# A GLU block beside memory attention on one core: the 64-row tail of each gate-up product held back and run as pairs on two halves of the TensorE array

## The chip, the core and the metric

The kernel runs on one core of a Trainium2 chip. A core has a matrix engine (TensorE, here PE, with its weight loads PEld), a vector engine (VectorE, DVE), a scalar engine (ScalarE, ACT), GpSimd (POOL) and SyncE (SP), whose queue issues most transfers between device memory and SBUF, the working memory of 128 partitions. Matmul results go to PSUM, which is used here as eight banks of 128 partitions by 512 float32. The metric is the time of one execution in microseconds on the device, smaller being better.

## The reference

```python
xn = _layernorm(x)
return x + _A_ref(xn, wq, wk, wv, wo, beta) + _B_ref(xn, w_gate, w_up, w_down)

# _B_ref: gated GLU, x [2048, 448], w_gate and w_up [448, 1792], w_down [1792, 448]
h = sigmoid(xn @ w_gate) * (xn @ w_up)
return h @ w_down
```

`_A_ref` is causal attention of 16 heads of 28 in four segments of 512 tokens, with a running memory of keys and values from the segments before, mixed by a learned gate and projected by `wo`. Everything is float32.

## The kernel before

Each float32 operand of a large product is split into a high part, in the type `float32r`, and the low rest. A product is then high by high, high by low and low by high. The contraction of 448 rows is three chunks of 128 and one of 64. The chunk of 64 is stored twice, one copy below the other, in a tile of 128 partitions: `xs[b][:, 3, :]` has the high part of the last 64 rows in partitions 0 to 63 and the low part in partitions 64 to 127, and the weights have their tail rows twice. So `TERMS` (line 53) has 11 matmuls: nine of the three full chunks, `(3, 3)`, which does high by high and high by low for the tail in one matmul, and `(3, 7)`, which multiplies the low weights with the tail. The tokens are four blocks of 512 (`b`).

The front of the program normalises the input, transposes it (`transpose_high`, `transpose_low`), and makes values, keys and queries. From then on two streams share the engines:

- `gated()` is the GLU. It takes the 14 slices of 128 hidden columns two at a time (`FG = 2`, from `f0`), and for each pair goes over the four token blocks: 28 group-blocks. A group-block has four slots, gate and up of slice `f0`, then gate and up of slice `f0 + 1`. A slot is one product of 11 matmuls of 128x512 into one PSUM bank (line 240). Gates go to the two banks tagged `gu`, ups to the two tagged `p`. After each up (slot 1 and slot 3) the gate is evaluated: ACT takes the tanh (line 248), DVE multiplies it with the up (249, which frees the `p` bank), ACT takes the high part (251) and DVE the low part (252) into `hh`.
- The products with `w_down` (`down`, line 161) wait in the list `todo`. After every slot one of them is popped: six matmuls of 128x448 (line 166) into a bank, and a DVE addition into `acc` (line 169), which frees the bank. The four downs of a group-block (`t` = 0 to 3) use the banks `pd`, `gu`, `pd`, `gu`.
- `attention()` runs in steps between them: score matmuls `st` (line 597, banks `s`), their copy on ACT, masking on POOL, maxima and subtraction on DVE, exponentials on ACT, and per unit of four heads the product `pa` with the values (line 672, the one bank `m`), which DVE transposes out of PSUM (line 675). The `pa` matmuls have 32 output columns each and four of them sit side by side in the array.

The order of PE and of SP's queue is written out by the program; the orders of DVE, ACT and POOL are made by the framework's scheduler. Every `yield` in `gated()` and `project()` lets a number of attention steps pass, spread evenly over all yields.

Weights of a slice come as one transfer of gate and up (`load_up`, tile `raw`, 128x1024, two buffers) and one of down (`load_down`, tile `rawd`, one buffer), and are split by ACT and DVE (`ready_up`, `ready_down`). The dictionary `ahead` says after which block and slot of a group each of these is issued.

After the GLU, `project()` multiplies the attention's output with `wo` and stores; what is left in `todo` runs there from `rest`.

Of the kernel before, what the change touches and what calls it, by code (L numbers as in the profile page):

```python
# [9 lines left out]
F32 = mybir.dt.float32  # L10
F32R = mybir.dt.float32r
AF = mybir.ActivationFunctionType
ALU = mybir.AluOpType
# [3 lines left out]
P = 128  # L17
D = 448
# [3 lines left out]
NB = 4  # L22
L = 512
NT = 4
F = 1792
NF = F // P
# [7 lines left out]
FG = 2  # L34
# [15 lines left out]

HIGH, LOW_X, LOW_W = ([(a + c, w + c) for c in range(3)] for a, w in ((0, 0), (4, 0), (0, 4)))
EARLY = [HIGH + LOW_X + [(3, 3)] + LOW_W + [(3, 7)], HIGH + LOW_W + LOW_X + [(3, 3), (3, 7)]]
TERMS = [t for c in range(3) for t in ((c, c), (c, 4 + c), (4 + c, c))] + [(3, 3), (3, 7)]
KS = 3 * DH
MANUAL = {mybir.EngineType.PE, mybir.EngineType.SP}
# [6 lines left out]
def kernel(  # L62
# [18 lines left out]
    xs = [keep.tile([P, 7, L], F32R, name=f"xs{b}") for b in range(NB)]  # L81
    acc = [keep.tile([P, NT, D], F32, name=f"acc{b}") for b in range(NB)]

    def split(hi, lo, src):
        A.activation(hi, src, AF.Copy)
        V.tensor_sub(lo, src, hi.bitcast(F32))
# [13 lines left out]
    def transpose_low(p3, dst, t):  # L100
        tok = slice(t * P, (t + 1) * P)
        V.tensor_sub(dst[:, 4:7, tok], p3[:, 0:3], dst[:, 0:3, tok].bitcast(F32))
        V.tensor_sub(dst[64:, 3, tok], p3[64:, 3], dst[64:, 3, tok].bitcast(F32))

    def transpose_split(pt, src, dst, t):
        transpose_low(transpose_high(pt, src, dst, t), dst, t)

    def x_block(b):
        return x[b * L:(b + 1) * L, :].rearrange("(t p) d -> p t d", p=P)
# [5 lines left out]
    def bank(name, tag):  # L115
        return ps.tile([P, L], F32, name=name, tag=tag, bufs=banks[tag])
# [22 lines left out]
    mid = ctx.enter_context(tc.tile_pool(name="mid", bufs=3, reuse_waits="tile"))  # L139
# [7 lines left out]
    def two_k(name):  # L147
        return mid.tile([P, L], F32, name=name, tag="2k", bufs=2)
# [10 lines left out]
    def gated():  # L159

        def down(b, hs, wd, t, tag="pd"):
            tok = slice(t * P, (t + 1) * P)
            mms = [(h[:, a, tok], wd[f][:, w, :]) for f, h in hs for a, w in ((0, 0), (0, 1), (1, 0))]
            pd = bank("pd", tag)
            for n, (l, r) in enumerate(mms):
                T.matmul(pd[:, :D], l, r, start=n == 0, stop=n == len(mms) - 1)  # L166
                if n == 2:
                    yield
            V.tensor_add(acc[b][:, t, :], pd[:, :D], acc[b][:, t, :])  # L169
            yield  # L170

        raw_up, raw_down, wgu, wdn = {}, {}, {}, {}

        def load_up(f):

            raw_up[f] = mid.tile([P, 1024], F32, name="raw", bufs=2)
            if f < NF:
                nc.sync.dma_start(raw_up[f], w_ffn[f][:, :1024])
            else:
                nc.sync.dma_start(raw_up[f][:, :2 * D], w_o[:, 2 * D * (f - NF):2 * D * (f - NF + 1)])  # L180

        def load_down(f, tag="rawd"):
            raw_down[f] = (mid.tile([P, 1024], F32, name="raw", bufs=2)[:, :D] if tag == "raw" else
                           mid.tile([P, D], F32, name="rawd", bufs=1))
            nc.sync.dma_start(raw_down[f], w_ffn[f][:, 1024:])

        def ready_up(f):
            wgu[f] = eight_k(F32R, "wgu")
            split_weights(wgu[f], raw_up[f].rearrange("p (c n) -> p c n", c=4))

        def ready_down(f):
            wdn[f] = late_pair("wdn")
            split(wdn[f][:, 0, :], wdn[f][:, 1, :], raw_down[f])

        def ready_out(h):
            wo[h] = eight_k(F32R, "wo").rearrange("p c n -> p (c n)")
# [12 lines left out]
        for f0 in range(0, NF, FG):  # L209


            ahead = {}
            if f0 == 0:
                ahead[0, 0] = lambda: (load_down(1, "raw"), ready_up(1))
                ahead[0, 2] = lambda: load_up(2)
                ahead[1, 3] = lambda: load_up(3)
            if f0 + FG < NF:
                ahead[1, 2] = lambda: ready_up(f0 + 2)
                if f0 > 0:
                    ahead[2, 1] = lambda: ready_down(f0 + 2)  # L220
                ahead[2, 3] = lambda: load_down(f0 + 3)
                ahead[2, 2] = lambda: load_up(f0 + 4)
                ahead[3, 2] = lambda: ready_up(f0 + 3)
                ahead[3, 3] = lambda: ready_down(f0 + 3)
                if f0 > 0:
                    ahead[0, 2] = lambda: (load_up(f0 + 3), load_down(f0 + 2))
            else:

                ahead[0, 2] = lambda: load_up(f0 + 3)
                ahead[1, 2] = lambda: ready_out(0)  # L230
                ahead[3, 2] = lambda: ready_out(1)
            for b in range(NB):
                hs = []
                for f in range(f0, f0 + FG):
                    pgu = []
                    for side in range(2):
                        slot = 2 * (f - f0) + side
                        dst = bank("pgu", ("gu", "p")[side])
                        for n, (a, w) in enumerate(TERMS):
                            T.matmul(dst, wgu[f][:, w, side * P:(side + 1) * P], xs[b][:, a, :],  # L240
                                     start=n == 0, stop=n == len(TERMS) - 1)
                            if n in (3, 7):
                                yield
                        pgu.append(dst)
                        if side == 1:

                            sg = two_k("sg")
                            A.activation(sg, pgu[0], AF.Tanh, scale=0.5)  # L248
                            V.scalar_tensor_tensor(sg, sg, 1.0, pgu[1], op0=ALU.add, op1=ALU.mult)  # L249
                            hh = four_k(F32R, "hh")  # L250
                            A.activation(hh[:, 0, :], sg, AF.Copy, scale=0.5)  # L251
                            V.scalar_tensor_tensor(hh[:, 1, :], sg, 0.5, hh[:, 0, :].bitcast(F32),  # L252
                                                   op0=ALU.mult, op1=ALU.subtract)
                            hs.append((f, hh))
                        yield
                        if todo and f0 + b > 0:
                            yield from todo.pop(0) or ()
                        if (b, slot) in ahead:
                            ahead[b, slot]()
                end = f0 + FG == NF and b == NB - 1  # L260
                todo += [down(b, hs, wdn, t, ("pd", "s" if end else "gu")[t % 2]) for t in range(NT)]
        rest.extend(todo)


    N_FFN = NF // FG * NB * 20 - 12


    with tc.tile_pool(name="front", bufs=2) as sb, tc.manual_schedule(engines=FRONT):
# [49 lines left out]
            return xn  # L318

        def turn(b, t, xn):  # L320
            transpose_split(bank("pt", "s"), xn, xs[b], t)

        def value_terms(b, t, pv, terms, n0=0, n1=len(TERMS)):
            for n in range(n0, n1):
# [112 lines left out]
            p3[t] = transpose_high(bank("pt", "s"), xn[t], xs[0], t)  # L437

        def turn_low(t):
            transpose_low(p3[t], xs[0], t)  # L440

        def normalised(t):
            xn[t] = normalise(0, t, *rstd(*st[t], y[t])[0])
# [49 lines left out]
        for b in range(NB):  # L493
# [24 lines left out]
            for k, c in enumerate((3, 4, 5, 6, 0, 1, 2) if last else range(7)):  # L518
# [215 lines left out]
    def project():  # L734

        def split_tokens(b, t):
            o3 = sums[b][:, :, t * P:(t + 1) * P]
            A.activation(xs[b][:, 0:4, t * P:(t + 1) * P], o3, AF.Copy)
            transpose_low(o3, xs[b], t)

        def out_weights(w):
            at = 2 * D * (w // 4) + D * (w % 2)
# [76 lines left out]
```

## Time and profile before

| What | Value |
|---|---|
| Time, median of 3 runs | 697.93 us (696.47, 697.93, 700.5) |
| Profiled execution, first to last instruction | 697.6 us |
| PE, PEld busy | 690.0 us, 567.7 us |
| DVE busy | 570.2 us |
| ACT, POOL busy | 343.6 us, 148.5 us |
| Gate-up products (line 240) | 1232 matmuls of 128x512 |
| Down products (line 166) | 672 matmuls of 128x448 |
| TensorE clock granted | 0.997 of full |

Matmuls overlap in the pipeline, so the busy time of one (398 ns for a 128x512 one) is longer than the distance from its start to the next one's. Rates are read from start to start. DVE, ACT and POOL work through their queues in order, so an instruction that waits holds up what stands behind it on its engine.

### The profile page before, as it was taken

The page shows a single profiled execution, that of the slowest core. Times are in us where ns is not written, and L with a number is a line of the kernel's source. Part 1 is how long each engine was busy: PE and PEld are TensorE (multiplying, and loading weights), DVE is VectorE, ACT ScalarE, POOL GpSimd, SP SyncE. Part 2 cuts the span into 40 slices and gives each one's busy share as a digit, 9 for nine tenths or more (in the row PEclk, how much of TensorE's full clock was granted, in tenths as well). Part 3 has the DMA queues.
Part 4 walks back from the last instruction along what each step waited for, and adds up shares of the span by engine and source line. Part 5 has one row for each costly group of instructions (what it writes and reads, how often), then busy time and mean ns, then how long its engine had stood idle before and what let it go on. Part 6 is the DMA issues. An engine that isn't in the chain of part 4 may idle for free.

```text
span 697.6 us, 10438 instructions
## 1 busy us (share of the span) xinstructions
PE 690.0 (99%) x3594; PEld 567.7 (81%) x3594; DVE 570.2 (82%) x994; ACT 343.6 (49%) x563; POOL 148.5 (21%) x349
## 2 busy tenths in 40 slices
PE   8989999999999999999999999999999999999997
PEld 7878878777878787877878778787787878778897
DVE  6665687658789898988898889998898889889863
ACT  5646646344455455543655446455644555446320
POOL 4400010101222131322222222132221322222000
PEclk9999999999999999999999999999999999999999
DMA  7833545687222423234323343324242432333342
GB/s 265 320 130 149 201 185 211 226 300 224 70 77 65 120 86 85 48 113 108 78 58 96 70 128 66 98 56 114 74 108 66 95 70 60 86 94 88 91 152 105
DMA packets 45797, 84.37 MB, mean 121 GB/s; under 512 B 6321, under 2 KB 20401, under 8 KB 45233
## 3 DMA queue, kind: packets, MB, share of 16 engines
q1 hardware_dynamic: 42736, 76.37, 35.3%
q0 software_dynamic: 3008, 7.34, 5.2%
q8 instruction: 28, 0.46, 0.3%
q14 instruction: 25, 0.20, 0.1%
HBM read 51.05 MB, written 32.64 MB: 120 GB/s over the span
## 4 chain that ended last, share of the span: by engine, by line
PE 94%; DMA 2%; DVE 1%; ACT 1%; SPq 0%; issue 0%; ACTq 0%
PE pgu L240 42%; PE pd L166 20%; PE pp L344 9%; PE st L597 5%; PE pa L672 5%; PE po L756 5%; PE pv L326 4%; PE pmm L372 2%; PE n L390 1%; DMA qd<-qk 1%; DMA acc<-in_x 1%; PE pt L95 1%; PE pk L364 1%; DVE stats L285 0%; ACT L512 0%
## 5 line engine op out<-in xcount | busy, mean ns | idle before, releaser
L240 PE MATMUL pgu<-xs,wgu 128*128 128x512 f32 x1232 | 321.0, 398 | 0.0
L240 PEld LDWEIGHTS pgu<-xs,wgu 128*128 128x128 f32 x1232 | 226.6, 188 | 48.0 <-issue 3.2
L166 PE MATMUL pd<-wdn,hh 128*128 128x448 f32 x672 | 162.4, 368 | 0.0
L612 POOL TENSOR_SCALAR_AFFINE_SELECT w<-w 128x256 f32<-128x256 f32 (+1 forms) x160 | 81.7, 512 | 254.1 <-ACT w L601 215.1
L166 PEld LDWEIGHTS pd<-wdn,hh 128*128 128x128 f32 x672 | 123.2, 188 | 15.1 <-issue 1.0
L652 ACT ACTIVATE w<-w 128x1024 f32<-128x1024 f32 (+1 forms) x96 | 87.1, 915 | 87.6 <-DVE w L651 87.0
L651 DVE TENSOR_TENSOR w<-w,mb 128x1024 f32<-128x1024 f32 (+1 forms) x96 | 99.7, 1049 | 0.2
L601 ACT ACTIVATE w<-st 128x512 f32<-128x512 f32 x128 | 75.0, 588 | 43.6 <-PE st L597 43.5
L614 DVE TRANSPOSE_TENSOR_REDUCE mx<-w 128x32 f32<-128x1024 f32 x64 | 79.1, 1235 | 12.7 <-POOL w L612 12.7
L344 PE MATMUL pp<-xs,wqk 128*128 128x512 f32 x308 | 80.6, 412 | 0.0
L344 PEld LDWEIGHTS pp<-xs,wqk 128*128 128x128 f32 x308 | 58.1, 192 | 14.8 <-issue 2.4
L169 DVE TENSOR_TENSOR acc<-pd,acc 128x448 f32<-128x448 f32 x112 | 67.4, 602 | 2.7 <-PE pd L166 2.5
L597 PE MATMUL st<-qk 84*128 84x128 f32 (+3 forms) x256 | 64.0, 311 | 0.0
L251 ACT ACTIVATE hh<-sg 128x512 fp32r<-128x512 f32 x56 | 35.1, 627 | 44.5 <-DVE sg L249 35.0
L597 PEld LDWEIGHTS st<-qk 84*128 84x128 f32 x256 | 48.4, 189 | 8.6 <-ACT w L601 0.2
L248 ACT ACTIVATE sg<-pgu 128x512 f32<-128x512 f32 x56 | 33.3, 594 | 40.1 <-PE pgu L240 40.1
L641 DVE STREAM_TRANSPOSE mb<-top 128x1024 f32<-128x1024 f32 x32 | 39.8, 1242 | 10.3 <-POOL top L638 10.1
L351 DVE TENSOR_TENSOR qk<-pp,qk 128x512 fp32r<-128x512 f32 x28 | 19.3, 688 | 34.6 <-ACT e L349 27.3
L249 DVE SCALAR_TENSOR_TENSOR sg<-sg,pgu 128x512 f32<-128x512 f32 x56 | 37.4, 668 | 4.8 <-PE pgu L240 4.8
L252 DVE SCALAR_TENSOR_TENSOR hh<-sg,hh 128x512 fp32r<-128x512 f32 x56 | 38.6, 690 | 2.7 <-ACT hh L251 2.5
L326 PE MATMUL pv<-wv,xs 128*128 128x448 f32 x176 | 39.7, 377 | 0.3
L672 PE MATMUL pa<-w,vv 128*32 128x128 f32 (+3 forms) x512 | 38.4, 436 | 0.0
(100 smaller groups left out, 639.2 us busy)
## 6 DMA issues: line engine op xcount, KB each, us to landing
qk<-qd SPq DMA_DIRECT2D x192, 112.0 KB
qd<-qk SPq DMA_DIRECT2D x28, 512.0 KB
raw<-in_w_ffn SPq DMA_DIRECT2D x14, 512.0 KB
vd<-vst SPq DMA_DIRECT2D x4, 1024.0 KB
vv<-vd SPq DMA_DIRECT2D x16, 256.0 KB
od<-w POOLq DMA_DIRECT2D x16, 256.0 KB, 4.0
sums<-od SPq DMA_DIRECT2D x32, 128.0 KB
out<-acc SPq DMA_DIRECT2D x16, 224.0 KB
```

Source lines behind the costliest of these rows:

```text
L166: T.matmul(pd[:, :D], l, r, start=n == 0, stop=n == len(mms) - 1)
L169: V.tensor_add(acc[b][:, t, :], pd[:, :D], acc[b][:, t, :])
L240: T.matmul(dst, wgu[f][:, w, side * P:(side + 1) * P], xs[b][:, a, :], start=n == 0, stop=n == len(TERMS) - 1)
L326: T.matmul(pv[:, :D], xs[b][:, a, t * P:(t + 1) * P], wv[w], start=n == 0, stop=n == len(TERMS) - 1)
L344: T.matmul(pp, wqk[c][:, w, :], xs[b][:, a, :], start=n == 0, stop=n == len(TERMS) - 1)
L597: T.matmul(st[:, at:at + L - kb * P], self.qk[:KS, 1, h, kb * P:(kb + 1) * P], self.qk[:KS, 0, h, kb * P:], start=True, stop=True)
L601: A.activation(w, st, AF.Copy)
L612: G.affine_select(d, d, pattern=pattern, base=0, channel_multiplier=-1, compare_op=ALU.is_ge, fill=MASK)
L614: V.tensor_reduce(mx[:, 16 * (n - 1):16 * (n + 1)], w3[:, n // 2, :2 * L].rearrange("p (b n) -> p b n", n=32), axis=mybir.AxisListType.X, ...
L651: V.tensor_sub(w, w, m)
L652: A.activation(w, w, AF.Exp, scale=SCALE)
L672: T.matmul(pa[32 * j:32 * j + 32, kb * P:], self.vv[:, kb, 32 * j:32 * j + 32], self.pairs[j // 2].block(j % 2, kb), start=kb == 0, stop=k ...
```

## The change

The matmul `(3, 7)` is taken out of the four slots. Each slot runs the first ten terms (`WHOLE = 10`) and leaves its bank open. At the end of slot 3 four matmuls of 64 rows follow, one for each of the four open banks, with the low tail weights and the high tail of `x`: gates on partitions 0 to 63, ups on partitions 64 to 127. The program gives them tiles of 64 rows by 128 columns, at rows 0, 64, 0, 64 of the array. Their other factor, low by low, is no longer computed. Only then are both gates evaluated, one behind the other.

For this the high tail of `x` must exist on both halves. Odd blocks keep the low part in partitions 0 to 63 (`low_rows`), and a new tile `xd` for each pair of blocks holds the missing copies, made by four GpSimd copies in the front. Two tiles of 2 KB per partition are added; `raw` goes from two buffers to one.

All of a group-block's downs now use other places and banks: two (`t` = 2, 3 of the block before) at the start of the group-block, one each after slots 1 and 2 (`t` = 0, 1), in the banks `pd`, `pd`, `pd`, `m`. Loads and splits of weights move to other slots.

```diff
+WHOLE = 10
...
+    xd = [keep.tile([P, L], F32R, name=f"xd{n}") for n in range(NB // 2)]
+    def low_rows(b):
+        return slice(64, P) if b % 2 == 0 else slice(0, 64)
+    def high_tail(b, side):
+        r = slice(64 * side, 64 * side + 64)
+        return xs[b][r, 3, :] if side == b % 2 else xd[b // 2][r, :]
...
-            raw_up[f] = mid.tile([P, 1024], F32, name="raw", bufs=2)
+            raw_up[f] = mid.tile([P, 1024], F32, name="raw", bufs=1)
...
-        begin.extend([lambda: ready_down(0), lambda: (ready_down(1), load_down(2)), lambda: ready_down(2)])
+        begin.extend([lambda: (ready_down(0), load_down(1)), lambda: None, lambda: (ready_down(1), load_down(2))])
...
             if f0 == 0:
-                ahead[0, 0] = lambda: (load_down(1, "raw"), ready_up(1))
-                ahead[0, 2] = lambda: load_up(2)
-                ahead[1, 3] = lambda: load_up(3)
+                ahead[0, 0] = lambda: ready_up(1)
+                ahead[0, 3] = lambda: ready_down(2)
+            ahead[0, 2] = lambda: load_up(f0 + 2)
+            ahead[1, 3] = lambda: load_up(f0 + 3)
             if f0 + FG < NF:
                 ahead[1, 2] = lambda: ready_up(f0 + 2)
                 if f0 > 0:
+                    ahead[0, 3] = lambda: load_down(f0 + 2)
                     ahead[2, 1] = lambda: ready_down(f0 + 2)
                 ahead[2, 3] = lambda: load_down(f0 + 3)
-                ahead[2, 2] = lambda: load_up(f0 + 4)
-                ahead[3, 2] = lambda: ready_up(f0 + 3)
-                ahead[3, 3] = lambda: ready_down(f0 + 3)
-                if f0 > 0:
-                    ahead[0, 2] = lambda: (load_up(f0 + 3), load_down(f0 + 2))
+                ahead[3, 2] = lambda: ready_down(f0 + 3)
+                ahead[3, 3] = lambda: ready_up(f0 + 3)
...
+                yield from due(2)
+                for slot in range(2 * FG):
+                    f, side = f0 + slot // 2, slot % 2
+                    dst = bank("pgu", ("gu", "p")[side])
+                    for n, (a, w) in enumerate(TERMS[:WHOLE]):
+                        T.matmul(dst, wgu[f][:, w, side * P:(side + 1) * P], xs[b][:, a, :],
+                                 start=n == 0, stop=False)
...
+                    if slot == 2 * FG - 1:
+                        for k in range(2 * FG):
+                            r = slice(64 * (k % 2), 64 * (k % 2) + 64)
+                            T.matmul(pgu[k], wgu[f0 + k // 2][r, 7, k % 2 * P:(k % 2 + 1) * P],
+                                     high_tail(b, k % 2), start=False, stop=True)
+                        for k in range(FG):
...
+                    if slot in (1, 2):
+                        yield from due(1)
...
-                todo += [down(b, hs, wdn, t, ("pd", "s" if end else "gu")[t % 2]) for t in range(NT)]
+                todo += [down(b, hs, wdn, t, ("pd", "s" if end else ("pd", "m")[t // 2])[t % 2])
+                         for t in range(NT)]
...
-    N_FFN = NF // FG * NB * 20 - 12
+    N_FFN = NF // FG * NB * 20 - 8
...
+            high = slice(64, P) if b % 2 else slice(0, 64)
+            G.tensor_copy(xd[b // 2][low_rows(b), :], xs[b][high, 3, :])
...
-    N_OUT = 1 + NB * NT * 3 + 12
+    N_OUT = 1 + NB * NT * 3 + 8
```

`due(n)` pops that many downs from `todo`; it does nothing in the first group-block.

More of the change, by code (lines that the diff above doesn't have):

```diff
@@ L98, in transpose_high, with transpose_low @@
         return p3
-    def transpose_low(p3, dst, t):
+    def transpose_low(p3, b, t):
+        dst, r = xs[b], low_rows(b)
         tok = slice(t * P, (t + 1) * P)
         V.tensor_sub(dst[:, 4:7, tok], p3[:, 0:3], dst[:, 0:3, tok].bitcast(F32))
-        V.tensor_sub(dst[64:, 3, tok], p3[64:, 3], dst[64:, 3, tok].bitcast(F32))
-    def transpose_split(pt, src, dst, t):
-        transpose_low(transpose_high(pt, src, dst, t), dst, t)
+        V.tensor_sub(dst[r, 3, tok], p3[r, 3], dst[r, 3, tok].bitcast(F32))
     def x_block(b):
@@ L180, in load_up, with load_down @@
                 nc.sync.dma_start(raw_up[f][:, :2 * D], w_o[:, 2 * D * (f - NF):2 * D * (f - NF + 1)])
-        def load_down(f, tag="rawd"):
-            raw_down[f] = (mid.tile([P, 1024], F32, name="raw", bufs=2)[:, :D] if tag == "raw" else
-                           mid.tile([P, D], F32, name="rawd", bufs=1))
+        def load_down(f):
+            raw_down[f] = mid.tile([P, D], F32, name="rawd", bufs=1)
             nc.sync.dma_start(raw_down[f], w_ffn[f][:, 1024:])
@@ L227, in gated @@
+                ahead[3, 3] = lambda: ready_up(f0 + 3)
             else:
-                ahead[0, 2] = lambda: load_up(f0 + 3)
                 ahead[1, 2] = lambda: ready_out(0)
-                ahead[3, 2] = lambda: ready_out(1)
+                ahead[3, 3] = lambda: ready_out(1)
             for b in range(NB):
[L233 to L245, printed above, removed]
+                hs, pgu = [], []
@@ new lines, in gated, with due @@
+                end = f0 + FG == NF and b == NB - 1
+                def due(n):
+                    for _ in range(n if todo and f0 + b > 0 else 0):
+                        yield from todo.pop(0) or ()
+                yield from due(2)
[5 more added lines that the diff above has]
+                                 start=n == 0, stop=False)
+                        if n in (3, 7):
+                            yield
+                    pgu.append(dst)
+                    if slot == 2 * FG - 1:
[4 more added lines that the diff above has]
+                        for k in range(FG):
@@ L247, in gated @@
                             sg = two_k("sg")
-                            A.activation(sg, pgu[0], AF.Tanh, scale=0.5)
-                            V.scalar_tensor_tensor(sg, sg, 1.0, pgu[1], op0=ALU.add, op1=ALU.mult)
+                            A.activation(sg, pgu[2 * k], AF.Tanh, scale=0.5)
+                            V.scalar_tensor_tensor(sg, sg, 1.0, pgu[2 * k + 1], op0=ALU.add, op1=ALU.mult)
                             hh = four_k(F32R, "hh")
@@ L253, in gated @@
                                                    op0=ALU.mult, op1=ALU.subtract)
[L254 to L260, printed above, removed]
-                todo += [down(b, hs, wdn, t, ("pd", "s" if end else "gu")[t % 2]) for t in range(NT)]
-        rest.extend(todo)
-    N_FFN = NF // FG * NB * 20 - 12
+                            hs.append((f0 + k, hh))
+                    yield
+                    if slot in (1, 2):
+                        yield from due(1)
+                    if (b, slot) in ahead:
+                        ahead[b, slot]()
+                todo += [down(b, hs, wdn, t, ("pd", "s" if end else ("pd", "m")[t // 2])[t % 2])
+                         for t in range(NT)]
+        for part in todo[:2]:
+            yield from part
+        rest.extend(todo[2:])
+    N_FFN = NF // FG * NB * 20 - 8
     with tc.tile_pool(name="front", bufs=2) as sb, tc.manual_schedule(engines=FRONT):
@@ L320, in turn @@
         def turn(b, t, xn):
-            transpose_split(bank("pt", "s"), xn, xs[b], t)
+            transpose_low(transpose_high(bank("pt", "s"), xn, xs[b], t), b, t)
         def value_terms(b, t, pv, terms, n0=0, n1=len(TERMS)):
@@ L439, in turn_low @@
         def turn_low(t):
-            transpose_low(p3[t], xs[0], t)
+            transpose_low(p3[t], 0, t)
         def normalised(t):
@@ L738, in split_tokens @@
             A.activation(xs[b][:, 0:4, t * P:(t + 1) * P], o3, AF.Copy)
-            transpose_low(o3, xs[b], t)
+            transpose_low(o3, b, t)
         def out_weights(w):
```

## The prediction

> **What bounds the kernel now.** I read the page first, then busy time by stage, the waits of PE and DVE, and last PE's timeline start by start.
>
> ```profile
> span 697.6 us, 10438 instructions
> PE 690.0 (99%) x3594; PEld 567.7 (81%) x3594; DVE 570.2 (82%) x994; ACT 343.6 (49%) x563; POOL 148.5 (21%) x349
> ...
> PE 94%; DMA 2%; DVE 1%; ACT 1%; SPq 0%; issue 0%; ACTq 0%
> ...
> L240 PE MATMUL pgu<-xs,wgu 128*128 128x512 f32 x1232 | 321.0, 398 | 0.0
> ...
> L248 ACT ACTIVATE sg<-pgu 128x512 f32<-128x512 f32 x56 | 33.3, 594 | 40.1 <-PE pgu L240 40.1
> ...
> L249 DVE SCALAR_TENSOR_TENSOR sg<-sg,pgu 128x512 f32<-128x512 f32 x56 | 37.4, 668 | 4.8 <-PE pgu L240 4.8
> L252 DVE SCALAR_TENSOR_TENSOR hh<-sg,hh 128x512 fp32r<-128x512 f32 x56 | 38.6, 690 | 2.7 <-ACT hh L251 2.5
> ```
> ```profile
> 0.00:155.00 155.00, 150.96 (x758) 126.79 (x759) 102.33 (x231) 81.21 (x151) 22.78 (x41) 0.99 0.60 219
> 155.00:650.00 495.00, 495.00 (x2600) 401.61 (x2599) 440.02 (x710) 254.53 (x399) 124.86 (x307) 1.00 0.35 89
> ```
> ```profile
> DVE mx L614 <- POOL w L612: 12.7, 26, 1.3
> DVE mx L634 <- POOL up L633: 10.3, 26, 0.7
> DVE mb L641 <- POOL top L638: 10.1, 18, 0.7
> DVE top L636 <- POOL up L635: 6.9, 23, 0.5
> DVE sg L249 <- PE pgu L240: 4.8, 4, 2.2
> DVE acc L169 <- PE pd L166: 1.9, 2, 1.3
> ```
> ```profile
> PE pmm L372 <- ACT kn L366: 2.1, 1, 2.1
> ```
>
> The chain of waits is 94% PE, and between 155 and 650 us, where the GLU runs, PE is never idle: the only long PE wait lies in the front. But DVE is nearly as full. Of 495 us it works 440 and waits 42 for POOL (first four rows), inside chains that DVE itself started for 27 of them; it waits for PE 6.7 us directly, and 12.7 more through the mask. So some 20 us in 495 is all that DVE can gain on PE. The kernel has two bounds a few per cent apart, and PE stays unbroken only because each bank has time to be emptied.
>
> PE's rates come from start to start:
>
> ```profile
> 301.63 1.09 PE L240 MATMUL pgu<-xs,wgu 128*128 128x512 f32 x4
> 302.56 0.40 PE L597 MATMUL st<-qk 84*128 84x512 f32 x1
> 302.80 1.39 PE L166 MATMUL pd<-wdn,hh 128*128 128x448 f32 x6
> 304.02 0.40 PE L597 MATMUL st<-qk 84*128 84x384 f32 x2
> ...
> 307.19 1.37 PE L166 MATMUL pd<-wdn,hh 128*128 128x448 f32 x6
> 308.40 2.02 PE L240 MATMUL pgu<-xs,wgu 128*128 128x512 f32 x8
> ...
> 312.09 0.77 PE L166 MATMUL pd<-wdn,hh 128*128 128x448 f32 x3
> 312.69 1.10 PE L240 MATMUL pgu<-xs,wgu 128*128 128x512 f32 x4
> ...
> 316.35 0.84 PE L166 MATMUL pd<-wdn,hh 128*128 128x448 f32 x3
> 317.03 1.10 PE L240 MATMUL pgu<-xs,wgu 128*128 128x512 f32 x4
> ```
>
> A gate-up matmul takes (302.56 - 301.63)/4 = 0.233 us, a down matmul (304.02 - 302.80)/6 = 0.203, a score chunk of 512 columns 0.24.
>
> **The tails.** Each of 28 group-blocks loses four full matmuls, 4 x 0.233 = 0.93 us, and gets four 64-row ones. No 64-row tile is in this trace; the nearest rows are `pa`, which has four tiles of 32 columns side by side.
>
> ```profile
> 266.03 1.09 PE L240 MATMUL pgu<-xs,wgu 128*128 128x512 f32 x4
> 267.06 2.36 PE L672 MATMUL pa<-w,vv 128*32 128x512 f32 x32
> 269.35 1.90 PE L240 MATMUL pgu<-xs,wgu 128*128 128x512 f32 x7
> 271.08 1.37 PE L166 MATMUL pd<-wdn,hh 128*128 128x448 f32 x6
> ```
> ```profile
> 269.01 0.40 PE L672 MATMUL pa<-w,vv 128*32 128x128 f32 x8
> ```
> ```profile
> L672 PE MATMUL pa<-w,vv x32: 272/444/617, 444.0 to 446.7; 128*32 128x512 f32 x8, 128*32 128x384 f32 x8, 128*32 128x256 f32 x8, 128*32 128x128 f32 x8
> L675 DVE STREAM_TRANSPOSE w<-pa x1: 696/696/696, 448.1 to 448.1; 128x512 f32<-128x512 f32 x1
> ```
>
> Side by side works: 32 matmuls in 2.29 us, 72 ns each, though each lasts 272 to 617 ns. So I take two pairs at 2 x 0.233 = 0.47 us. Changing the tiling is not free. Going in: 267.06 - 266.03 is 1.03 us for four matmuls worth 0.93, so 0.10. Coming out: the last eight `pa` take 0.34 us to the next start, while the 24 before took 1.95 us for 2 x (512 + 384 + 256) columns, which makes 0.22 for 2 x 128: 0.12 more. And the seven products after it take 1.73 us where 7 x 0.233 = 1.63: another 0.10. One round trip is 0.32 us. The first pair's weights of 128 columns cannot be in the array before the change; between nothing and the 0.10 just seen, I take 0.05. The tails then cost 0.47 + 0.32 + 0.05 = 0.84 us, a gain of 0.09 per group-block and 2.5 us in all. Bounds: with no cost of changing, 0.47 less, 13 us gained; with the four one after another plus 0.42, 12 us lost.
>
> The Trainium skill (TensorE: Matmul & The Clock Gate, "Measured speedup vs the span model") gives 3.07 for four row tiles, not 4. By that, as an estimate, two pairs take 4 x 0.233 x 1/1.53 = 0.61 us in place of 0.47, and the sum would be 4 us higher. This trace's `pa` shows no such loss for column tiles (four tiles of 512 columns inside the first 617 ns); for row tiles it has no row.
>
> **Banks and waits.** All four banks now end together, and both evaluations (2 x 0.668 + 2 x 0.690 = 2.7 us of DVE) fall into one place instead of two. Tanh frees the `gu` banks 0.6 us later; the 12 down matmuls at the start of the next group-block (2.4 us) cover that. The first `p` bank is wanted after 2.4 + 2.3 us and a score chunk or two; the DVE product behind tanh is usually done by then. In group-block 1 there are no downs yet, and slot 0 meets tanh: 1 us once.
>
> The downs have less room. `t` = 0, 1, 2 share one bank. In the changed order, between `t` = 0 and `t` = 1 stand ten gate-up matmuls and about one score chunk, 2.33 + 0.24 = 2.57 us; between `t` = 1 and `t` = 2 the tails more, 3.4 us. DVE must have done the addition in that time. How late is it now?
>
> ```profile
> 306.19 0.59 DVE L169 TENSOR_TENSOR acc<-pd,acc 128x448 f32<-128x448 f32 x1
> ...
> 310.46 0.61 DVE L169 TENSOR_TENSOR acc<-pd,acc 128x448 f32<-128x448 f32 x1
> ...
> 313.93 0.62 DVE L169 TENSOR_TENSOR acc<-pd,acc 128x448 f32<-128x448 f32 x1
> ...
> 319.94 0.58 DVE L169 TENSOR_TENSOR acc<-pd,acc 128x448 f32<-128x448 f32 x1
> ```
>
> Against the downs that ended (next start on PE) at 304.02, 308.40, 312.69 and 317.03, the additions ended 2.76, 2.67, 1.86 and 3.49 us later, 2.70 on average. At these lags PE waits 0.19, 0.10, 0 and 0.92 us before `t` = 1, 0.30 on average, and nearly nothing before `t` = 2: 28 x 0.3 = 8.4 us. Behind the waiting matmul stand all later products and scores, and with the scores the attention's work on DVE.
>
> Bank `m`: `t` = 3 and `pa` now alternate on it. In the changed order three `pa` stand 0.6, 0 and 1.2 us of PE work ahead of a `t` = 3, and three stand 1.0, 0 and 0.9 us behind one. In the unit quoted above the last `pa` starts at 446.7 us, some 0.2 before PE goes on, and the transpose that frees `m` ends at 448.1 + 0.7: 1.9 us. So 1.3 + 1.9 + 0.7 and, with the addition's 2.7, 1.7 + 2.7 + 1.8: 10 us.
>
> Together 18 us at today's lags; below, nothing, if the waits let DVE catch up, since a backlog is paid once. I take 10, the middle: after each wait DVE is ahead by it at the next bank, but on average it regains only 20 us in 28 group-blocks, 0.7 us each, and the bunched 2.7 us of evaluation renews the lag in every one.
>
> **Edits at nothing.** `raw` with one buffer: 0.5 MB at the 89 GB/s of this stage is 6 us, against four slots (17 us) to its split; SP may stand for the split before issuing a load, with the score operands of the next pair behind it, wanted some 15 us later. Without that cover it is some us at 7 places. The split of slice f0 + 3 moves behind the tails; PE wants it two slots and 18 downs later, 8.3 us, and DVE needs 2.7 of lag, 2.7 of evaluation and 1.2. The `xd` copies lie on POOL, busy 23 of the front's 155 us. The two downs that move out of the output stage cost the same there.
>
> **Sum**: 697.6 - 2.5 + 1 + 10 = 706.1 in the profiled execution's time; the median of the runs is 0.3 above its span: 706.
>
> **Rivals.**
> 1. *Changing to 64-row tiles costs nothing* (faster). The tiles keep all columns, which `pa` does not, so PE might not have to empty. Against it: nothing here shows it. 13 us gained, and then DVE is the bound sooner: with 1 + 4 of waits, 690. It decides if the tails take under 0.5 us from start to start. Chance 0.17.
> 2. *The waits don't come.* The scheduler lays DVE's order anew, and additions early in it would keep the lag under 2.57 us; three of four lags above are near that. 697.9 - 2.5 + 1 = 696. Chance 0.2.
> 3. *The change doesn't do what it says*: the pairs run one after another. PE is then slower by 12, covers grow, waits shrink to 4: 715. `pa` speaks against it. Chance 0.1.
>
> My forecast, waits at the banks that eat a small gain: 0.53, between 700 and 712. A measurement of this kernel tells 0.5% (3.5 us) from no change. Faster by more than that: rival 1 and a little of 2, 0.18. Within: most of 2 and the lower edge of mine, 0.22. Slower: 0.60. The range reaches down into rival 1 and up to rival 3: 692 to 716.
>
> **What would show it.** Right: the four tail matmuls as two pairs of starts some ns apart, 0.8 us from first tail to the next full product after taking off what follows; a list of PE waits that now names the additions on `pd` and the transposes on `m`, some 10 us; DVE's waits for PE above 6.7 us. Wrong: tails in 0.5 us; no PE waits for DVE; a PE wait for tanh or for the evaluation's product in every group-block (then the `p` bank, not the downs, is the tight place, and the time lies above 710); score matmuls waiting for transfers.

## The result, and the profile after

The changed kernel takes 733.9 us (median of 4 runs, 733.7 to 735.3), the kernel before 697.3: slower, ratio 1.053 with a 95% interval of 1.0512 to 1.0548. The forecast was 706, in a range of 692 to 716. The sign was right, the size was not: 36.6 us where 8 were expected.

The page of the changed kernel, against the lines shown of before:

```profile
span 732.3 us, 10443 instructions
PE 696.6 (95%) x3594; PEld 554.4 (76%) x3594; DVE 570.4 (78%) x994; ACT 341.7 (47%) x563; POOL 150.3 (21%) x353
...
PE 58%; DVE 14%; issue 12%; POOL 6%; DMA 4%; ACT 4%; SPq 1%; POOLq 0%; ACTq 0%; DVEq 0%
...
L250 PE MATMUL pgu<-xs,wgu 128*128 128x512 f32 x1120 | 295.7, 402 | 1.4 <-ACT sg L263 1.4
...
L174 PE MATMUL pd<-wdn,hh 128*128 128x448 f32 x672 | 162.8, 373 | 15.9 <-DVE acc L177 9.9
...
L616 PE MATMUL st<-qk 84*128 84x128 f32 (+3 forms) x256 | 65.2, 316 | 0.9 <-ACT w L620 0.9
...
L691 PE MATMUL pa<-w,vv 128*32 128x256 f32 (+3 forms) x512 | 41.2, 455 | 10.2 <-issue 10.2
```

The number to see is the idle time behind the bar: 1.4 + 15.9 + 0.9 + 10.2 = 28.4 us, where the gate-up and down groups of before had 0.0. DVE has done the same work (570 us), and ACT and POOL are within 2 us of theirs. PE's busy time is 6.6 us higher, though it has less to do; the paragraph on what makes up 34.7 us, below, says why. The chain of waits, 94% PE before, is now handed between PE, DVE, POOL and ACT.

The list of waits of the same run (waiter, releaser, total, times, longest):

```profile
DVE mx L633 <- POOL w L631: 29.8, 28, 2.8
...
DVE acc L177 <- PE pd L174: 12.4, 10, 2.2
...
PE pa L691 <- issue: 10.2, 4, 3.8
PE pd L174 <- DVE acc L177: 9.9, 9, 2.0
...
PE pd L174 <- DVE w L694: 5.8, 3, 2.3
```

PE waits for DVE and DVE waits for PE, each more than before: over the whole run DVE's waits for downs went from 2.5 to 12.4 us, those for masks, which come from PE's scores through ACT and POOL, from 12.7 to 29.8. When PE stands, no scores are made, and a little later DVE stands too. Three PE waits are for the transpose of `pa` in bank `m`. The four for "issue" before `pa` have no named releaser in the list; the timeline of one gives it.

```profile
331.26 0.77 PE L174 MATMUL pd<-wdn,hh 128*128 128x448 f32 x3
331.87 1.10 PE L250 MATMUL pgu<-xs,wgu 128*128 128x512 f32 x4
336.37 2.36 PE L691 MATMUL pa<-w,vv 128*32 128x512 f32 x32 [3.40 <-issue]
```
```profile
331.35 0.69 DVE L267 SCALAR_TENSOR_TENSOR hh<-sg,hh 128x512 fp32r<-128x512 f32 x1 [0.70 <-ACT hh L266]
331.96 0.68 DVE L264 SCALAR_TENSOR_TENSOR sg<-sg,pgu 128x512 f32<-128x512 f32 x1
332.56 0.61 DVE L177 TENSOR_TENSOR acc<-pd,acc 128x448 f32<-128x448 f32 x1
333.32 1.25 DVE L633 TRANSPOSE_TENSOR_REDUCE mx<-w 128x32 f32<-128x1024 f32 x1
334.49 0.65 DVE L267 SCALAR_TENSOR_TENSOR hh<-sg,hh 128x512 fp32r<-128x512 f32 x1
335.06 0.70 DVE L637 TRANSPOSE_TENSOR_REDUCE mx<-w 128x16 f32<-128x512 f32 x1
335.68 0.58 DVE L177 TENSOR_TENSOR acc<-pd,acc 128x448 f32<-128x448 f32 x1
```

The last down of `t` = 3 ended on PE at 331.87 (next start) and its addition at 336.26, 4.4 us later; `pa`, which needs the same bank `m`, starts at 336.37. Between them DVE did the rest of the double evaluation, the addition of `t` = 2 and two maxima of the attention. This is the changed order in small: an addition that frees a bank stands behind the evaluation of two slices.

The tails themselves, in PE's timeline around 350 us:

```profile
350.12 0.68 PE L250 MATMUL pgu<-xs,wgu 128*128 128x512 f32 x2
350.74 0.49 PE L259 MATMUL pgu<-xs,wgu 64*128 64x512 f32 x1
350.74 0.50 PE L259 MATMUL pgu<-xd,wgu 64*128 64x512 f32 x1
351.07 0.39 PE L259 MATMUL pgu<-xs,wgu 64*128 64x512 f32 x1
351.08 0.39 PE L259 MATMUL pgu<-xd,wgu 64*128 64x512 f32 x1
...
351.39 1.49 PE L174 MATMUL pd<-wdn,hh 128*128 128x448 f32 x6
352.72 0.40 PE L616 MATMUL st<-qk 84*128 84x256 f32 x2
```

The two of a pair start within some ns of each other, so they run side by side. The first pair takes 0.33 us to the second, the second 0.32 to the next start, instead of 0.233; and the six downs behind it take 1.33 instead of 1.22. From the start of the last full matmul to the first tail are 0.326 us (median of the 28 places), 0.09 more than 0.233. Together that is 0.09 + 0.33 + 0.32 + 0.11 = 0.85 us for what took 4 x 0.233 = 0.93.

### The profile page after: what moved, and what is told of

Its sections match the earlier page's. It is cut to its first block, busy times and chain, and to the rows that moved or that the text cites. A ratio compares the mean times of both kernels' runs of the same rounds, so it can differ in the third digit from the quotient of the medians.

```text
span 732.3 us, 10443 instructions
## 1 busy us (share of the span) xinstructions
PE 696.6 (95%) x3594; PEld 554.4 (76%) x3594; DVE 570.4 (78%) x994; ACT 341.7 (47%) x563; POOL 150.3 (21%) x353
## 4 chain that ended last, share of the span: by engine, by line
PE 58%; DVE 14%; issue 12%; POOL 6%; DMA 4%; ACT 4%; SPq 1%; POOLq 0%; ACTq 0%; DVEq 0%
PE pgu L250 20%; PE pd L174 11%; PE pp L361 8%; PE po L775 5%; POOL w L631 4%; PE pa L691 3%; PE pv L343 3%; PE st L616 3%; DVE mx L633 3%; DVE w L670 2%; DVE acc L177 2%; DVE mb L660 1%; PE pgu L259 1%; PE pmm L389 1%; DVE hh L267 1%
## 5 line engine op out<-in xcount | busy, mean ns | idle before, releaser
L250 PE MATMUL pgu<-xs,wgu 128*128 128x512 f32 x1120 | 295.7, 402 | 1.4 <-ACT sg L263 1.4
L250 PEld LDWEIGHTS pgu<-xs,wgu 128*128 128x128 f32 x1120 | 207.8, 190 | 47.4 <-issue 3.2
L174 PE MATMUL pd<-wdn,hh 128*128 128x448 f32 x672 | 162.8, 373 | 15.9 <-DVE acc L177 9.9
L174 PEld LDWEIGHTS pd<-wdn,hh 128*128 128x128 f32 x672 | 120.7, 188 | 39.3 <-DVE acc L177 15.3
L631 POOL TENSOR_SCALAR_AFFINE_SELECT w<-w 128x256 f32<-128x256 f32 (+1 forms) x160 | 80.1, 502 | 277.7 <-ACT w L620 231.2
L633 DVE TRANSPOSE_TENSOR_REDUCE mx<-w 128x32 f32<-128x1024 f32 x64 | 79.2, 1238 | 29.9 <-POOL w L631 29.8
L361 PE MATMUL pp<-xs,wqk 128*128 128x512 f32 x308 | 79.0, 405 | 0.0
L177 DVE TENSOR_TENSOR acc<-pd,acc 128x448 f32<-128x448 f32 x112 | 67.2, 602 | 12.7 <-PE pd L174 12.4
L691 PE MATMUL pa<-w,vv 128*32 128x256 f32 (+3 forms) x512 | 41.2, 455 | 10.2 <-issue 10.2
L263 ACT ACTIVATE sg<-pgu 128x512 f32<-128x512 f32 x56 | 30.5, 593 | 30.9 <-PE pgu L259 30.9
L368 DVE TENSOR_TENSOR qk<-pp,qk 128x512 fp32r<-128x512 f32 x28 | 19.2, 687 | 32.2 <-ACT e L366 26.1
L691 PEld LDWEIGHTS pa<-w,vv 128*32 128x32 f32 x512 | 17.1, 113 | 35.5 <-issue 31.1
L264 DVE SCALAR_TENSOR_TENSOR sg<-sg,pgu 128x512 f32<-128x512 f32 x56 | 35.9, 673 | 4.6 <-ACT sg L263 3.3
```

The source lines that it names most:

```text
L361: T.matmul(pp, wqk[c][:, w, :], xs[b][:, a, :], start=n == 0, stop=n == len(TERMS) - 1)
L631: G.affine_select(d, d, pattern=pattern, base=0, channel_multiplier=-1, compare_op=ALU.is_ge, fill=MASK)
L633: V.tensor_reduce(mx[:, 16 * (n - 1):16 * (n + 1)], w3[:, n // 2, :2 * L].rearrange("p (b n) -> p b n", n=32), axis=mybir.AxisListType.X, ...
L691: T.matmul(pa[32 * j:32 * j + 32, kb * P:], self.vv[:, kb, 32 * j:32 * j + 32], self.pairs[j // 2].block(j % 2, kb), start=kb == 0, stop=k ...
```

## The experiments

Each run was timed against the kernel before on the same chip. The table is a ladder from the kernel before to the changed one, with one step added per row.

| Kernel | Median, us | Ratio to before, 95% interval |
|---|---|---|
| before (in that job) | 697.4 | |
| + new places of the downs (i_places_only) | 696.2 | 0.9985 [0.9966, 1.0005] |
| + three of four downs on `pd`, the fourth on `gu` (n_gu_for_m) | 708.0 | 1.0171 [1.0126, 1.0216] |
| + the fourth on `m` (c_downs_only) | 718.7 | 1.0298 [1.024, 1.0356] |
| + one raw buffer, new loads (b_eval_each) | 720.0 | 1.0319 [1.0277, 1.0362] |
| + four banks held, both slices evaluated together (a_full_rows) | 731.4 | 1.0479 [1.0444, 1.0514] |
| + tails as 64-row pairs (the changed kernel) | 733.9 | 1.053 [1.0512, 1.0548] |

### The ladder

**a_full_rows**: the tails as full matmuls at the same place.

```diff
-                            T.matmul(pgu[k], wgu[f0 + k // 2][r, 7, k % 2 * P:(k % 2 + 1) * P],
-                                     high_tail(b, k % 2), start=False, stop=True)
+                            T.matmul(pgu[k], wgu[f0 + k // 2][:, 7, k % 2 * P:(k % 2 + 1) * P],
+                                     xs[b][:, 3, :], start=False, stop=True)
```

> The four held tails run as matmuls of 128 rows, as before the change, at the place where the changed kernel has its pairs; everything else is the changed kernel. Theory 'waits at the downs' banks': the 64-row tiles have little to do with the 36 us, so this is within 4 us of the changed kernel (733.9): PE pays 0.93 us in place of 0.85 in each of 28 group-blocks, +2 us, 730 to 738. Rival 'changing the tiling costs far more than its starts show': 705 or less. Rival 'holding four banks': no difference either, 730 to 738.

731.4 us, as both theories said. PE's idle time stays: the groups of this run's page,

```profile
L690 PE MATMUL pa<-w,vv 128*32 128x128 f32 (+3 forms) x512 | 40.4, 451 | 10.0 <-issue 10.0
```

show the same 10 us before `pa`. The 64-row tiles bear no part of the loss worth naming. By their starts they gain 28 x 0.08 = 2 us; in the total the kernel with them is 2.5 slower. The intervals of the two ratios just overlap, and the granted clock differs too (0.992 to 0.998 in the runs with full rows, 0.991 to 0.993 with pairs), so this small difference stays open.

**b_eval_each**: eleven terms in each slot, each slice evaluated after its own up; downs, banks and loads of the changed kernel.

```diff
-                    for n, (a, w) in enumerate(TERMS[:WHOLE]):
+                    for n, (a, w) in enumerate(TERMS):
...
-                    if slot == 2 * FG - 1:
-                        for k in range(2 * FG):
...
-                        for k in range(FG):
+                    if side == 1:
+                        for k in [slot // 2]:
```

> The changed kernel without held tails: each slot runs its 11 terms and each slice is evaluated after its own up, as before; places and banks of the downs, the loads and the single raw buffer stay. Theory 'waits at the downs' banks': most of the loss stays, 715 to 733. Rival 'holding four banks and evaluating both slices together': 697 to 706.

720.0: of the 36 us, 22.6 stay and 11.4 go with the joint evaluation (to a_full_rows). The theory of the downs' banks holds for two thirds, and the rival for a third. Of the rival's two halves it is the evaluation that counts: PE's waits at the held banks themselves (for tanh) are 1.9 us in a_full_rows.

**c_downs_only**: the same, with two raw buffers and the old loads, that is, the kernel before with the downs' places and banks alone.

> The kernel before with the downs alone changed (two at the start, one after slots 1 and 2, banks pd, pd, pd, m); two raw buffers and the old places of loads. Theory 'waits at the downs' banks': 712 to 730, and within 4 us of the run that evaluates each slice (loads cost nothing). Rival 'holding four banks': 697 to 704.

718.7, 1.2 us from the run above. **d_loads_only** is the other side, the kernel before with one raw buffer and the new loads alone:

> The kernel before with one raw buffer and the new places of loads and splits alone. All theories but one: 697 plus or minus 2. Rival 'a transfer or a split comes late': over 702, with PE waits for a weight split or DVE and ACT waits for the raw transfer.

699.3, ratio 1.0016 [0.9998, 1.0034]. By both comparisons the loads cost 1 to 2 us, hardly above the noise.

**i_places_only** takes run c and gives the downs their old banks:

```diff
-("pd", "s" if end else ("pd", "m")[t // 2])[t % 2]
+("pd", "s" if end else "gu")[t % 2]
```

> The kernel before with the downs' new places alone (two at the start, one after slots 1 and 2), in the old banks pd and gu in turn. With the run that changes places and banks at 718.7 and the one that changes banks alone (all on pd) at 709.8, theory 'the short covers on pd and the sharing of m' gives 697 to 704 here; rival 'two downs in a row are the trouble, whatever their bank' gives 712 to 720.

696.2, no different from the kernel before. Two downs in a row cost nothing when they go to different banks with time behind them. So the 22 us of run c are the banks'. **n_gu_for_m** divides them, with `gu` in place of `m` for `t` = 3 alone:

> The run with the downs' new places and banks alone (718.7: pd, pd, pd, m), with the bank gu in place of m for t = 3. It takes bank m away from the downs and leaves pd with three of them. By that run's PE waits (3.5 us before t = 3 and 4.2 before the attention's product, of 18) theory 'pd and m each cost what their waits show' gives 708 to 714; rival 'm is nearly all of it' 697 to 704; rival 'm is nothing' 716 to 721.

708.0, at the lower edge of what the first theory gave: some 12 us are `pd`'s and some 11 `m`'s. PE's idle time shows the same in the pages of the two runs, first this one, then c_downs_only:

```profile
L173 PE MATMUL pd<-wdn,hh 128*128 128x448 f32 x672 | 160.1, 370 | 7.5 <-DVE acc L176 7.5
...
L686 PE MATMUL pa<-w,vv 128*32 128x128 f32 (+3 forms) x512 | 37.8, 436 | 0.0
```
```profile
L173 PE MATMUL pd<-wdn,hh 128*128 128x448 f32 x672 | 161.8, 372 | 11.5 <-DVE acc L176 8.1
...
L686 PE MATMUL pa<-w,vv 128*32 128x128 f32 (+3 forms) x512 | 39.9, 454 | 3.3 <-issue 3.3
```

With `m` free the waits before `pa` and for its transpose are gone, and those for the additions on `pd` stay at 8.

### Whether the banks or the joint evaluation work alone

**e_pd_only**: the kernel before, all downs on `pd`, one after every slot.

```diff
-("pd", "s" if end else "gu")[t % 2]
+("pd", "s" if end else "pd")[t % 2]
```

> The kernel before with all downs in the one bank pd, still one after every slot, so that 11 gate-up matmuls (2.6 us) lie between one addition and the next down. The additions of the kernel before end 2.7 us after their down on average. Theory 'waits at the downs' banks': slower, by the lag's excess over 2.6 us in 112 places, 705 to 720. Rival 'holding four banks': 697 to 702.

709.8, ratio 1.0163 [1.0123, 1.0202]. One short bank without anything else of the change costs 12 us.

**l_hold_pd** was to add the joint evaluation to it, with the evaluations of both slices written after slot 3.

```diff
+                        if side == 1:
+                            pend.append((f, pgu))
+                        for f_, pgu_ in (pend if slot == 2 * FG - 1 else ()):
                             sg = two_k("sg")
```

> The run with all downs on pd (709.8), and on top of it both slices evaluated together after slot 3, with full matmuls: holding without bank m and without 64-row tiles. Theory 'the evaluation of both slices at once makes DVE's additions later at every bank': 716 to 726. Rival 'holding costs only through bank m, where t = 3 and the attention's product meet': 706 to 714.

710.3, the rival's number, but the run does not test it. ACT and DVE are ordered by the scheduler, and the first slice's banks were complete after slot 1: in the trace DVE's two products of a group-block start 7.8 us apart (median; 8.8 in e_pd_only), while in the changed kernel they start 0.6 apart. The evaluation was written later and ran at the old time.

**m_hold_true** holds the banks by their data: the eleventh matmul of all four comes after slot 3.

```diff
-                        for n, (a, w) in enumerate(TERMS):
+                        for n, (a, w) in enumerate(TERMS[:10]):
...
+                        open_.append((dst, f, side))
+                        for d_, f_, s_ in (open_ if slot == 2 * FG - 1 else ()):
+                            T.matmul(d_, wgu[f_][:, 7, s_ * P:(s_ + 1) * P], xs[b][:, 3, :], start=False, stop=True)
```

> The run with all downs on pd, one after every slot (709.8), and on top of it the four eleventh matmuls held to the end of slot 3 as full 128-row ones, so that neither slice can be evaluated before. The run before this one meant to do that but left the first slice free to be evaluated early, and it was (its two evaluations lie 8.5 us apart). Here the additions that follow the end of a group-block should come later: theory 'the double evaluation delays the next additions at whatever bank they free' gives 716 to 728, with PE waits before the second down after the evaluation; rival 'holding costs only through bank m' gives 706 to 714.

730.3, ratio 1.047 [1.0429, 1.0511]: 20 us above e_pd_only, a little over the first theory's range and far from the rival's. No down touches bank `m` here, so the joint evaluation delays additions wherever the next down needs their bank:

```profile
L166 PE MATMUL pd<-wdn,hh 128*128 128x448 f32 x672 | 166.2, 374 | 19.6 <-DVE acc L169 19.2
```

The same line in e_pd_only:

```profile
L166 PE MATMUL pd<-wdn,hh 128*128 128x448 f32 x672 | 164.2, 371 | 9.0 <-DVE acc L169 9.0
```

**h_after_spread**: the changed kernel with downs at the start and after slots 0, 1 and 2, all on `pd`.

```diff
-                yield from due(2)
+                yield from due(1)
...
-                    if slot in (1, 2):
+                    if slot in (0, 1, 2):
```

> The changed kernel with its downs spread again: one at the start and one each after slots 0, 1 and 2, all in the bank pd, so that bank m is left to the attention's product. Theory 'bank m and two downs in a row make most of the loss': 706 to 722. Rival 'the pd bank, or holding four banks': 728 to 740.

735.3, no gain: what `m` gives back, `pd` takes. PE's waits before downs rise from 15.9 to 26.3 us, and 19 of them lie before the down that follows slot 0, whose bank must be freed by the addition that stands right behind the double evaluation.

### The tiling alone

**j_pair_per_slice**: the kernel before with one pair of tails after each up, so that each slice is evaluated at once and the downs stay as they were (one raw buffer and the new loads, for room).

```diff
+                        if side == 1:
+                            for k in range(2):
+                                r = slice(64 * k, 64 * k + 64)
+                                T.matmul(pgu[k], wgu[f][r, 7, k * P:(k + 1) * P], high_tail(b, k), start=False, stop=True)
```

> The kernel before with one pair of 64-row tails after each up, so that only two banks stay open, each slice is evaluated at once, and downs stay as they were (one after every slot, pd and gu in turn); one raw buffer and the new loads, as the copies of x need the room. It isolates the tiling: 56 changes there and back in place of 28. By the starts in the changed kernel's trace a pair costs 0.09 in, 0.32 and 0.10 out, 0.51 us, against 2 x 0.233 = 0.47 for the full matmuls: 56 x 0.04 = 2 us lost, and 2 for the loads: 699 to 705. Rival 'the tiling hurts DVE, ACT or the scheduler's order beyond its own starts': over 708. Rival 'the pairs gain': under 697.

709.9, above the range and where the rival put it. The starts explain most of it; I had priced a lone pair with the 0.32 us of a second pair:

```profile
303.67 0.40 PE L244 MATMUL pgu<-xs,wgu 128*128 128x512 f32 x1
304.00 0.49 PE L252 MATMUL pgu<-xs,wgu 64*128 64x512 f32 x1
304.00 0.49 PE L252 MATMUL pgu<-xd,wgu 64*128 64x512 f32 x1
304.42 0.50 PE L605 MATMUL st<-qk 84*128 84x512 f32 x1
304.76 0.77 PE L173 MATMUL pd<-wdn,hh 128*128 128x448 f32 x3
```

A lone pair pays both the first pair's extra 0.10 and the way out: 0.33 - 0.233 in, 0.42 for the pair, and 0.34 for a score chunk of 0.24 behind it: 0.10 + 0.42 + 0.10 = 0.62 us in place of 2 x 0.233 = 0.47. That is 56 x 0.15 = 8.6 us. The page has 2.5 us more of PE waits for tanh, in five places, which the kernel before does not have, and with 1 to 2 for the loads this makes the 12.5. So the pairs need each other: here one change there and back must carry at least two pairs, and the pairs then bind four banks.

### Is it DVE's load?

**f_before_pool** and **g_after_pool** take the low part of `hh` from DVE to GpSimd, in the kernel before and in the changed one.

```diff
-                            V.scalar_tensor_tensor(hh[:, 1, :], sg, 0.5, hh[:, 0, :].bitcast(F32),
-                                                   op0=ALU.mult, op1=ALU.subtract)
+                            G.tensor_sub(hh[:, 1, :], sg, hh[:, 0, :].bitcast(F32))
```

> The kernel before with the low part of hh subtracted on GpSimd in place of DVE (the factor 0.5 goes into the down weights): DVE loses 56 x 0.69 = 39 us of work, GpSimd gains some 72. PE has no waits to lose, so 695 to 699, if GpSimd does not hold up the masks (then up to 710).

> The changed kernel with the same: the low part of hh on GpSimd. Theory 'the additions and transposes come late because DVE is full': with 39 us less on DVE the waits shrink by more than half, 700 to 717. Rival 'DVE's order and the round trips, not its load': 725 to 738.

716.0 and 754.9, both outside what was expected, and both 18 to 21 us slower than their own base. In f_before_pool the 39 us of subtractions are gone from DVE, but its busy time falls by 12 us only (570.2 to 558.3), since other DVE instructions took longer (last section). It waits longer for masks, and PE now waits for scores' copies:

```profile
DVE mx L615 <- POOL w L613: 38.0, 40, 2.7
...
PE st L598 <- ACT w L602: 9.1, 10, 1.6
```

The test does not settle whether a freer DVE would have absorbed the waits: DVE was hardly freed, and GpSimd stands in the attention's chain and became late itself. Neither the theory of DVE's load nor its rival is shown by it.

## Why the prediction failed in size

**PE's gain: right.** 2.5 us were forecast from `pa`'s rows (0.84 us for a tail section), 0.85 us was measured. The pairs run side by side, and changing the tiling takes most of the gain, as in the sum. The Trainium skill (TensorE: Matmul & The Clock Gate, "Measured speedup vs the span model") has 3.07 for four row tiles, from which the prediction's estimate made 0.61 us for the two pairs; 0.33 + 0.32 us from first tail to next start was measured. That is near the estimate, but includes part of the change of tiling, and the trace does not separate the two.

**The sites: right.** Additions on `pd` before `t` = 1, the bank `m` in both directions. Of PE's 28.4 us of idle time in the changed kernel 26.1 lie at these places. The table has, for each, the forecast at the lags of the kernel before; the same sum over all places in the trace of i_places_only, which has the new order but no shared bank to wait for (the end of each addition or transpose less the start of what would need its bank in the changed kernel, where that is above nothing); and PE's idle time in two runs, all in us.

| PE's wait before | Forecast at the lags of before | Excess in i_places_only | Idle in c_downs_only | Idle in the changed kernel |
|---|---|---|---|---|
| `t` = 1 | 8.4 | 9.3 | 6.6 | 8.1 |
| `t` = 2 | nearly nothing | 4.9 | 1.5 | 2.0 |
| `t` = 3 | 3.9 | 5.8 | 3.4 | 5.8 |
| `pa` | 6.2 | 7.6 | 3.3 | 10.2 |
| Sum | 18 | 28 | 14.8 | 26.1 |

That the first forecast came out so near is partly luck: it counted too little, as the third column shows, and DVE regained part of that while PE waited.

**The step that failed: "Together 18 us at today's lags; below, nothing ... I take 10, the middle."** The term was mis-sized: 10 us were taken, 26.1 us of idle time was measured at these places, and the time rose by more than the idle time. Three things were wrong in it.

First, 18 was too small, because it stood on four lags. The long lags make the sum: in the kernel before, the 112 additions end 0.8 to 5.3 us after their downs, and their excess over 2.57 us is 0.45 us on average, 12.6 us in 28 places, not 8.4. In i_places_only seven places of 27 make up the 9.3 us before `t` = 1. At one of them PE starts a down (`t` = 0) and then the next one, which goes to another bank there, while DVE's addition of the first comes late:

```profile
475.01 1.40 PE L173 MATMUL pd<-wdn,hh 128*128 128x448 f32 x6
...
479.34 0.76 PE L173 MATMUL pd<-wdn,hh 128*128 128x448 f32 x3
```
```profile
480.48 0.61 DVE L176 TENSOR_TENSOR acc<-pd,acc 128x448 f32<-128x448 f32 x1
```

The addition ends at 481.09, 1.75 us after the second down has started.

The halving itself was not far off for the banks alone: of 28 us of excess, c_downs_only shows 14.8 as idle time, so DVE does regain something while PE waits. But the regain has a limit that the text named ("with the scores the attention's work on DVE") and did not price: DVE's own waits for downs and masks rose from 15.2 us before to 42.2 in the changed kernel, because its further work comes from PE.

Second, the joint evaluation was treated as covered (tanh, the `p` bank) and as a reason that the lag renews itself, not as a term. Measured as the end of the addition less the last down matmul's start and 0.203 us, averaged over 23 group-blocks, the additions of `t` = 2 and 3, which come right after the evaluation, went from 2.40 and 2.67 us before to 3.05 and 3.53; in b_eval_each, with the same banks and no joint evaluation, they were 2.35 and 2.49. (These two downs belong to the group-block before the one just evaluated, so they do not wait for its result.) The waits of PE before `t` = 3 and `pa` go from 6.5 us in b_eval_each to 15.0 in a_full_rows. In time the joint evaluation is worth 11 us on top of these banks and 20 in m_hold_true.

Third, the sum took a wait at its idle time; the next paragraph shows what else it costs.

**What makes up 34.7 us of span.** PE's idle time is 28.4. The slower clock after waits adds 4.5 (last section). In each of 22 waits the matmul's busy time of 0.40 us also hides 0.17 that is normally overlapped, 4 us. The tails give 2 back. The 1 us that was forecast for tanh is among the idle time (1.4 on the page).

**At nothing: right.** Raw buffer, loads, copies and places cost 1 to 2 us together, which these runs hardly tell from nothing.

One reading was off without effect: DVE's waits for POOL are 40 us by the four rows that the prediction shows, not 42.

**The rivals.** The one with the cheap change of tiling and the one in which pairs run one after another are refuted by the starts. "The waits don't come" is refuted by the page. The case that the forecast left out was its own mechanism at full size and above: the range ended at 716, since rival 3 gave 715 and the full 18 us would have given 714.

What stays open: how much of the loss another order on DVE would save. The scheduler makes that order, and each of these kernels has its own; steps of 1 or 2 us in the ladder may be such differences.

## What to carry to other kernels

When PE is unbroken and the engine that empties its banks is nearly full, price a change first by the time each bank has to be emptied: take the consumer's lag from the trace, compare it with the PE work between release and reuse, and add up the excess over all places, not an average of a few, since the long lags make it. Be slow to discount it for catching up if the consumer's further work comes from the waiting engine: here the full excess was 28 us, and the banks alone cost 22.5 us of time (i_places_only to c_downs_only). A joint evaluation lengthens the lag of whatever stands behind it, so a saving that needs several banks open at once has to beat that too; here 0.08 us per group-block stood against more than a microsecond.

To delay work whose order a scheduler makes, delay its data: written later in the program alone, it runs at the old time.

## What the runs showed of the hardware

After some of PE's waits the granted clock fell. The stages around the wait that ended at 275.47 us in the changed kernel (length, then busy time of PE, PEld, DVE, ACT, POOL, then clock, DMA share and GB/s):

```profile
270.00:275.00 5.00, 3.18 (x36) 1.42 (x35) 4.49 (x10) 1.40 (x3) 1.72 (x4) 1.00 0.70 166
275.40:277.00 1.60, 1.53 (x7) 1.38 (x7) 1.60 (x4) 0.00 (x0) 0.00 (x0) 0.86 0.03 10
277.00:281.00 4.00, 4.00 (x13) 3.17 (x12) 3.61 (x6) 2.55 (x3) 0.90 (x2) 0.63 0.00 0
281.00:285.00 4.00, 4.00 (x21) 3.40 (x20) 1.25 (x1) 2.31 (x5) 0.97 (x3) 1.00 0.17 66
```

13 matmuls fit into the 4 us at 0.63, 21 into the next 4. The same was seen at the waits of PE that ended at 527.84 us (2.2 us long; 0.63 from 528 to 532.5) and at 588.44 (3.9 us; 0.50 from 588 to 594), but not at those that ended at 336.37 (3.4 us; 1.00 from 336.3 to 340) and 677.09 (2.0 us; 1.00 from 677 to 681). So a wait can cost more than its length, and its length alone does not tell whether it will: the mean clock of the run is 0.991 against 0.997, and 732.3 x 0.009 less 697.6 x 0.003 is 4.5 us. The Trainium skill (TensorE: Matmul & The Clock Gate, "What's actually happening") says that the clock gate halves the rate after an idle window of about 3.4 us; here an idle stretch of 2.3 us was followed by a lower clock, and one of 3.4 us was not.

The subtraction of 128x512 that DVE does in 0.69 us took GpSimd 1.44 (f_before_pool), and in the same run DVE's own subtractions of the maxima rose from 1.05 to 1.17 us on average:

```profile
L254 POOL TENSOR_TENSOR hh<-sg,hh 128x512 fp32r<-128x512 f32 x56 | 80.4, 1436 | 103.2 <-ACT hh L253 102.5
```
```profile
L652 DVE TENSOR_TENSOR w<-w,mb 128x1024 f32<-128x1024 f32 (+1 forms) x96 | 110.6, 1167 | 0.2
```
